# First x block and first two gates loaded and worked in halves, in a SwiGLU feed-forward kernel

## The chip, the cores and the metric

The kernel runs on one core of a Trainium2 chip. A time is that of one execution on the device in microseconds (us). The span in a profile runs from the first to the last instruction of the program, and times inside an execution are counted from the span's start.

## The reference

```python
B, S, D, F = 1, 2048, 512, 1376        # bf16; x, w_gate, w_up, w_down normal * 0.05

def reference(x, w_gate, w_up, w_down):
    g = silu(x @ w_gate)               # [S, F]
    u = x @ w_up                       # [S, F]
    return (g * u) @ w_down            # [S, D]
```

## The kernel before

Everything is held on chip. `xT_sb` has x transposed, as 4 blocks of 128 values of D (`dk` 0 to 3) by 2048 tokens; `w_sb` has the gate and up weights, `wd_sb` the down weights. F = 1376 is cut into 10 blocks of 128 (`ft`) and a rest of 96; the tokens are cut into 4 chunks of 512 (`SC`).

For each chunk and block there is one gate group G and one up group U, each a PSUM bank of 128 x 512 that sums over the 4 blocks of D. A 128-column weight block is worked as two 64-column halves side by side in the array (`m` 0 and 64), so matmuls come in pairs that run at the same time. ScalarE takes silu of G out of PSUM (L291), VectorE multiplies it with U (L305) into `hT_sb`. The rest of 96 is done in groups X and Y (L409, L420). Then the down projection runs over `hT_sb` (L456, L433) and the result is stored. The order of every engine's work is written out by hand: lists of groups, of ScalarE and of VectorE operations, with one counting semaphore for each of TensorE (`s_P`), ScalarE (`s_A`) and VectorE (`s_D`), and one semaphore for each load. `need(name)` makes TensorE wait for a load, `after(...)` for a ScalarE or VectorE operation.

What surrounds the change is the start:

- SP issues the loads in this order: `xn`, the first 256 tokens of x untransposed (256 KB, `HT` = 256); `wu0`, up columns 0 to 255 (256 KB); `x0b` and `x0c`, the next two 128 tokens by a transposing DMA; then slabs of gate and up weights, later chunks of x, and the down weights. ScalarE issues one load first of all: `wg0`, gate columns 0 to 255 (256 KB).
- TensorE runs `N_WARM` = 6 matmuls of constants, 512 wide (L359), and `N_FILL` = 2 pairs of 128 wide (L364). Then it waits for `xn` and transposes it: per block of D four transposes of 64 x 64 into a PSUM view `tview(dk)` for blocks 0 to 2 (L374), and four of 128 rows by 64 columns for the last block (L382). VectorE copies blocks 0 and 2 to `xT_sb`, ScalarE blocks 1 and 3 (L309, L291).
- Then come the first groups, on the first 256 tokens: gates 0 and 1 (`g0`, `g1`) block by block of D, 16 matmuls of 256 columns in all; ups 0 and 1 (`u0`, `u1`), 16 more; then `g0` on the tokens of `x0b` and `x0c`, the others on the rest. All these are L345.

`xn` holds tokens 2p and 2p + 1 in partition p, so that a token half of 128 is a half of 64 partitions. The list `turn` says which PSUM bank each group takes.

## Time and profile before

| | |
|---|---|
| time, median of 3 runs | 119.6 us (119.53 to 120.37) |
| time of the profiled execution | 120.67 us |
| its span | 119.3 us |
| TensorE (PE) busy | 116.6 us, 98% of the span |
| VectorE (DVE) busy | 43.4 us |
| ScalarE (ACT) busy | 35.5 us |
| granted TensorE clock | 1.00 |
| L345 matmuls | 680, 71.0 us |
| L359 and L364, matmuls of constants | 10, from 0.77 to 3.8 us |

The profile's chain of work is followed back from the last instruction, at each step to what released it. PE is TensorE's matmuls, PEld its weight loads, which lie beside them; SPq and ACTq are the queues of SP and ScalarE, whose lines show the issue of a DMA and not its transfer. A group's line has engine, operation, output and inputs with their shape, and the count. TensorE's first matmul starts 0.77 us after the span's start.

### The profile page before, as it was taken

The numbers are of one execution on the slowest core, as the hardware profiler recorded it, in microseconds if no ns is written. First come the engines' busy times: TensorE is split into PE (matmuls) and PEld (weight loads), VectorE is DVE, ScalarE is ACT, GpSimd is POOL, SyncE is SP. The second block draws the span as 40 slices with busy tenths as digits, with TensorE's granted clock in tenths as the row PEclk, the third lists the DMA queues.
The fourth block names the chain that finished last, engine by engine and source line by source line (L and its number), as shares of the span: only waits on it lengthen the run. The fifth ranks groups of instructions, "written<-read, shape, count | busy, mean of one in ns | idle before, by whom it ended". The sixth has DMA issues, their size and how long they took to land.

```text
span 119.3 us, 2992 instructions
## 1 busy us (share of the span) xinstructions
PE 116.6 (98%) x1343; PEld 66.4 (56%) x1344; DVE 43.4 (36%) x68; ACT 35.5 (30%) x61; POOL 0.4 (0%) x5
## 2 busy tenths in 40 slices
PE   7999999999999999999999999999999999999993
PEld 2796555555555555555555555554444444464452
DVE  0103534442534452444352444369800040214331
ACT  4225243265242365232454323470000030213001
POOL 1000000000000000000000000000000000000000
DMA  3999999991000000000000000000000023023612
GB/s 80 278 283 335 194 253 228 269 295 23 0 5 0 0 0 0 5 0 5 0 5 0 0 0 0 5 0 0 5 0 5 0 86 95 0 92 106 204 44 88
DMA packets 17596, 8.92 MB, mean 75 GB/s; under 512 B 8624, under 2 KB 17456, under 8 KB 17584
## 3 DMA queue, kind: packets, MB, share of 16 engines
q1 hardware_dynamic: 16912, 8.38, 27.1%
q10 hardware_dynamic: 672, 0.36, 1.0%
q8 instruction: 10, 0.16, 0.6%
q14 instruction: 2, 0.02, 0.0%
HBM read 4.81 MB, written 2.10 MB: 58 GB/s over the span
## 4 chain that ended last, share of the span: by engine, by line
PE 98%; issue 0%; DVE 0%
PE psum L345 59%; PE psum L456 24%; PE psum L433 7%; PE psum L409 3%; PE psum L359 2%; PE psum L420 1%; PE psum L382 0%; PE psum L374 0%; PE psum L364 0%; DVE o_sb L309 0%; PE psum L508 0%
## 5 line engine op out<-in xcount | busy, mean ns | idle before, releaser
L345 PE MATMUL psum<-xT_sb,w_sb 128*64 128x512 bf16 (+2 forms) x680 | 71.0, 371 | 0.0
L345 PEld LDWEIGHTS psum<-xT_sb,w_sb 128*64 128x64 bf16 x680 | 43.0, 112 | 27.1
L305 DVE TENSOR_TENSOR hT_sb<-sg_sb,psum 128x512 bf16<-128x512 f32 x40 | 27.5, 687 | 41.5 <-PE psum L345 36.6
L291 ACT ACTIVATE sg_sb<-psum 128x512 f32<-128x512 f32 x40 | 23.8, 596 | 41.6 <-PE psum L345 41.6
L456 PE MATMUL psum<-wd_sb,hT_sb 32*128 32x512 bf16 x480 | 26.9, 374 | 0.0
L456 PEld LDWEIGHTS psum<-wd_sb,hT_sb 32*128 32x128 bf16 x480 | 13.0, 93 | 13.0 <-issue 0.4
L309 DVE CAST o_sb<-psum 128x512 bf16<-128x512 f32 (+1 forms) x11 | 6.4, 603 | 25.2 <-PE psum L456 19.9
L291 ACT ACTIVATE o_sb<-psum 128x512 bf16<-128x512 f32 (+1 forms) x7 | 3.7, 580 | 33.0 <-PE psum L456 25.9
L433 PE MATMUL psum<-wd_sb,hT_sb 128*128 128x512 bf16 (+2 forms) x59 | 8.7, 307 | 0.2 <-issue 0.2
L433 PEld LDWEIGHTS psum<-wd_sb,hT_sb 128*128 128x128 bf16 x60 | 4.6, 98 | 4.6 <-issue 0.4
L305 DVE TENSOR_TENSOR ht_sb<-sgy_sb,yu_sb 32x512 bf16<-32x512 f32 x8 | 5.5, 683 | 0.4
L409 PE MATMUL psum<-xT_sb,w_sb 128*64 128x512 bf16 x32 | 4.2, 379 | 0.0
L305 DVE TENSOR_TENSOR ht_sb<-sgx_sb,psum 32x512 bf16<-32x512 f32 x4 | 2.8, 691 | 3.5 <-ACT sgx_sb L291 3.5
L291 ACT ACTIVATE sgx_sb<-psum 32x512 f32<-32x512 f32 x4 | 2.4, 588 | 4.5 <-PE psum L409 4.5
L359 PE MATMUL psum<-const-bfloat16-1.0 128*128 128x512 bf16 x6 | 2.7, 623 | 0.8 <-PEq L531 0.8
L456 PE MATMUL psum<-wdt_sb,ht_sb 32*128 32x512 bf16 (+1 forms) x48 | 3.3, 371 | 0.0
L409 PEld LDWEIGHTS psum<-xT_sb,w_sb 128*64 128x64 bf16 x32 | 2.0, 110 | 1.4
L291 ACT ACTIVATE sgy_sb<-psum 64x512 f32<-64x512 f32 x4 | 2.4, 590 | 0.1
L456 PEld LDWEIGHTS psum<-wdt_sb,ht_sb 32*128 32x128 bf16 x48 | 1.3, 93 | 1.3
L420 PE MATMUL psum<-xT_sb,w_sb 128*64 128x512 bf16 x16 | 1.9, 379 | 0.0
L359 PEld LDWEIGHTS psum<-const-bfloat16-1.0 128*128 128x128 bf16 x6 | 0.7, 133 | 1.9 <-issue 1.9
L280 ACT ACT_TABLE_LOAD x1 | 1.3, 1283 | 1.2 <-PEq L531 1.2
(21 smaller groups left out, 7.6 us busy)
## 6 DMA issues: line engine op xcount, KB each, us to landing
out_dram<-o_sb SPq DMA_DIRECT2D x15, 128.0 KB, 1.8
wd_sb<-in_w_down_dram SPq DMA_DIRECT2D x1, 1280.0 KB, 8.9
w_sb<-in_w_up_dram SPq DMA_DIRECT2D x4, 256.0 KB, 4.0
w_sb<-in_w_gate_dram SPq DMA_DIRECT2D x3, 256.0 KB, 3.9
wdt_sb<-in_w_down_dram SPq DMA_DIRECT2D x4, 96.0 KB, 7.2
w_sb<-in_w_gate_dram SPq DMA_DIRECT2D x1, 352.0 KB, 6.2
w_sb<-in_w_up_dram SPq DMA_DIRECT2D x1, 320.0 KB, 6.3
w_sb<-in_w_gate_dram ACTq DMA_DIRECT2D x1, 256.0 KB, 3.6
```

Source lines behind the costliest of these rows:

```text
L280: act.activation(adummy[:, 0:4], zero_c, ACT.Silu)
L291: act.activation(op["out"], op["src"], fn).then_inc(s_A, 1)
L305: ins = dve.tensor_tensor(op["out"], op["a"], op["b"], ALU.mult)
L309: ins = dve.tensor_copy(op["out"], op["src"])
L345: ins = pe.matmul(g["bank"][m:m + HC, n0:n1], lhsT=w_sb[:, dk, col + m:col + m + HC], rhs=xT_sb[:, dk, c * SC + n0:c * SC + n1], start=(dk ...
L359: pe.matmul(banks[NB - 1][:, 0:width], lhsT=ones_w, rhs=ones_m[:, 0:width], start=True, stop=True)
L409: ins = pe.matmul(g["bank"][m:m + HC, :], lhsT=w_sb[:, dk, XC0 + m:XC0 + m + HC], rhs=xT_sb[:, dk, c * SC:(c + 1) * SC], start=(dk == 0), ...
L420: ins = pe.matmul(g["bank"][y0:y1, :], lhsT=w_sb[:, dk, YC0:YC0 + 64], rhs=xT_sb[:, dk, c * SC:(c + 1) * SC], start=(dk == 0), stop=(dk == ...
L433: ins = pe.matmul(g["bank"][:, 0:c1 - c0], lhsT=hT_sb[:, fk, t * P:(t + 1) * P], rhs=wd_sb[:, fk, c0:c1], start=(start and fk == 0), stop= ...
L456: ins = pe.matmul(g["bank"][:, 0:c1 - c0], lhsT=h(r, g["t"]), rhs=w[R * r:R * (r + 1), c0:c1], start=(start and n == 0), stop=final, tile_ ...
```

## The change

The load of the first 256 tokens becomes two loads of 64 partitions (128 tokens, 128 KB each): `xn0` on SP in the old place, `xn1` on ScalarE's queue. The load `wg0` becomes `wg0a` (blocks 0 and 1 of D, 128 KB) and `wg0b` (blocks 2 and 3), both on ScalarE's queue, with `xn1` between them. `wu0` and all later loads keep their place on SP.

TensorE runs 4 matmuls of 512 and 3 pairs of 128 of constants. It then transposes the first half (8 transposes of 64 x 64), runs gates 0 and 1 on it for blocks 0 and 1 of D, transposes the second half, runs the gates on the first half for blocks 2 and 3, and then on the second half for all four. The gate matmuls of this part are 32 of 128 columns. The copies to `xT_sb` are one for each half and block: VectorE takes the first half's four and two of the second's, ScalarE the other two. All 4 blocks use the 64 x 64 form, and the list of banks is rearranged for it.

```diff
-N_WARM = 6
-N_FILL = 2
+N_WARM = 4
+N_FILL = 3
...
-        turn = [0, 2, 1, 3, 4, 5, 6, 7]
+        turn = [0, 4, 2, 6, 1, 3, 5, 7]
...
+        def load_rows(eng, h):
+            eng.dma_start(
+                xn_sb[h * HC:(h + 1) * HC, :, :].rearrange("p j d -> p (j d)"),
+                xf[h * P:(h + 1) * P, :].rearrange("(p j) d -> p (j d)", j=NXN),
+            ).then_inc(load_sem(f"xn{h}"), 16)
+
+        KH = KD // 2
...
         def loads_on_scalar(act):
-            load_w(act, "wg0", w_gate, 0, 0, slabs[0][1] * P)
+            load_w(act, "wg0a", w_gate, 0, 0, slabs[0][1] * P, 0, KH)
+            load_rows(act, 1)
+            load_w(act, "wg0b", w_gate, 0, 0, slabs[0][1] * P, KH, KD)
 
         def loads_on_sync(sp):
-            sp.dma_start(
-                xn_sb[:, :, :].rearrange("p j d -> p (j d)"), xf[0:HT, :].rearrange("(p j) d -> p (j d)", j=NXN)
-            ).then_inc(load_sem("xn"), 16)
+            load_rows(sp, 0)
             load_w(sp, "wu0", w_up, UPH, 0, slabs[0][1] * P)
             load_x(sp, "x0b", HT, HT + P)
...
+        def half(ap, h):
+            return ap.rearrange("p (i h t) -> p h i t", i=NXN, h=2)[:, h]
...
-        for dk in range(KD):
-            g = add_group("T", dk=dk)
-            eng = "DA"[dk % 2]
...
+        for h in range(2):
+            for dk in range(KD):
+                g = add_group("T", dk=dk)
+                eng = "A" if h and dk % 2 else "D"
+                op = add_op(
+                    eng, g, kind="copy", out=half(xT_sb[:, dk, 0:HT], h), src=tview(dk)[:, h], stored=(None, 0),
+                )
+                xt_ready[h, dk] = (eng, op["at"])
...
+            def transposes(h):
+                need(f"xn{h}")
+                if h == 0:
+                    pe.wait_ge(s_J, 1)
+                t0 = h * HC
+                for dk in range(KD):
+                    for i in range(NXN):
                         ins = pe.transpose(
                             tview(dk)[:, h, i, :], xn_sb[t0:t0 + HC, i, dk * P:(dk + 1) * P],
                             ident[t0:t0 + HC, t0:t0 + HC],
                         )
...
+                    ins.then_inc(s_P, 1)
+
+            def gate_part(h, dk0, dk1):
+                for g in (g0, g1):
+                    for dk in range(dk0, dk1):
+                        need("wg0a" if dk < KH else "wg0b")
+                        after(*xt_ready[h, dk])
+                        col = g["ft"] * P
+                        for m in (0, HC):
+                            pe.matmul(
+                                half(g["bank"][m:m + HC, 0:HT], h), lhsT=w_sb[:, dk, col + m:col + m + HC],
+                                rhs=half(xT_sb[:, dk, 0:HT], h), start=(dk == 0), stop=(dk == KD - 1),
+                                tile_position=(0, m),
+                            )
 
             g0, u0, g1, u1 = groups[NT:NT + 4]
-            for dk in range(KD):
-                for g in (g0, g1):
-                    gu_step(g, dk, 0, HT)
+            transposes(0)
+            gate_part(0, 0, KH)
+            transposes(1)
+            gate_part(0, KH, KD)
+            gate_part(1, 0, KD)
             for g in (u0, u1):
                 gu_matmuls(g, 0, HT)
```

More of the change, by code (lines that the diff above doesn't have):

```diff
@@ L95, in load_x, with load_w @@
             ).then_inc(load_sem(name), 16)
-        def load_w(eng, name, src, base, f0, f1):
+        def load_w(eng, name, src, base, f0, f1, k0=0, k1=KD):
             eng.dma_start(
-                w_sb[:, :, base + f0:base + f1],
-                src[:, f0:f1].rearrange("(k p) f -> p k f", p=P),
+                w_sb[:, k0:k1, base + f0:base + f1],
+                src[k0 * P:k1 * P, f0:f1].rearrange("(k p) f -> p k f", p=P),
             ).then_inc(load_sem(name), 16)
+        def load_rows(eng, h):
[4 more added lines that the diff above has]
+        KH = KD // 2
         slabs = [(0, 2), (2, 4), (4, 6), (6, 8), (8, NFT)]
@@ L140, in add_group @@
         def add_group(kind, **what):
-            g = dict(kind=kind, at=len(groups), bank=banks[turn[(len(groups) - KD) % NB]], readers=[], **what)
+            g = dict(kind=kind, at=len(groups), bank=banks[turn[(len(groups) - 2 * KD) % NB]], readers=[], **what)
             groups.append(g)
@@ L154, in tview @@
             return psum[:, 2 * dk:2 * dk + 2, 0:HC].bitcast(BF16).rearrange("p h (i t) -> p h i t", i=NXN)
-        def tview_last():
-            return psum[:, 6, 0:P].bitcast(BF16).rearrange("p (i t) -> p i t", i=NXN)
+        def half(ap, h):
+            return ap.rearrange("p (i h t) -> p h i t", i=NXN, h=2)[:, h]
         sg_reader = []
@@ L218, in bass_standalone__swiglu_ffn__prompt_kernel @@
         xt_ready = {}
-        for dk in range(KD):
-            g = add_group("T", dk=dk)
-            eng = "DA"[dk % 2]
-            out = xT_sb[:, dk, 0:HT]
-            if dk < KD - 1:
-                out, src = out.rearrange("p (i h t) -> p h i t", i=NXN, h=2), tview(dk)
-            else:
-                out, src = out.rearrange("p (i t) -> p i t", i=NXN), tview_last()
-            op = add_op(eng, g, kind="copy", out=out, src=src, stored=(None, 0))
-            xt_ready[dk] = (eng, op["at"])
+        for h in range(2):
[6 more added lines that the diff above has]
+                xt_ready[h, dk] = (eng, op["at"])
         NT = len(groups)
@@ L339, in gu_step @@
                     need("x0c")
-                need(("wg" if g["kind"] == "G" else "wu") + str(slab_of[ft]))
-                if c == 0 and n0 < HT:
-                    after(*xt_ready[dk])
+                side = ("a" if dk < KH else "b") if g["kind"] == "G" and slab_of[ft] == 0 else ""
+                need(("wg" if g["kind"] == "G" else "wu") + str(slab_of[ft]) + side)
                 col = (0 if g["kind"] == "G" else UPH) + ft * P
@@ L367, in on_tensor @@
                     )
-            need("xn")
-            pe.wait_ge(s_J, 1)
-            for dk in range(KD - 1):
-                for i in range(NXN):
-                    for h in range(2):
-                        t0 = h * HC
+            def transposes(h):
[5 more added lines that the diff above has]
+                    for i in range(NXN):
                         ins = pe.transpose(
@@ L377, in on_tensor @@
                         )
-                ins.then_inc(s_P, 1)
-            for i in range(NXN):
-                for m in (0, HC):
-                    c0 = (KD - 1) * P + m
-                    ins = pe.transpose(tview_last()[m:m + HC, i, :], xn_sb[:, i, c0:c0 + HC], ident[:, :])
-            ins.then_inc(s_P, 1)
-            g0, u0, g1, u1 = groups[NT:NT + 4]
-            for dk in range(KD):
-                for g in (g0, g1):
-                    gu_step(g, dk, 0, HT)
+                    ins.then_inc(s_P, 1)
[11 more added lines that the diff above has]
+                            )
+            g0, u0, g1, u1 = groups[NT:NT + 4]
+            transposes(0)
[3 more added lines that the diff above has]
+            gate_part(1, 0, KD)
             for g in (u0, u1):
```

## The prediction

> **What bounds the kernel now.** I read the page's chain first, then the chain in order of time, then the timeline of the first 9 us, then the DMA answers for short windows of the start.

> The chain, in order of time (start us, us, what):

> ```profile
> PE 98%; issue 0%; DVE 0%
> ...
> 0.77 2.72 PE psum L359 x6
> 3.49 0.33 PE psum L364 x3
> 3.82 0.33 PE psum L374 x11
> 4.15 0.36 PE psum L382 x4
> 4.51 18.56 PE psum L345 x200
> ```

> TensorE is the bound from 0.77 us to the end, without a hole. So the change can pay only in the first 6 us, where TensorE does work that isn't the result (L359, L364) because the loads aren't there yet. Everything later keeps its instructions and their order.

> The timeline of the start (start us, us, engine, line). The last five lines, from narrow windows, are pairs of weight loads of 256-column matmuls:

> ```profile
> 0.73 0.46 ACTq L98 DMA_DIRECT2D w_sb<-in_w_gate_dram  x1
> 0.74 0.41 SPq L114 DMA_DIRECT2D xn_sb<-in_x_dram  x1
> 1.20 0.41 SPq L98 DMA_DIRECT2D w_sb<-in_w_up_dram  x1
> 3.65 0.50 PE L374 MATMUL psum<-ident,xn_sb 64*128 64x64 bf16 x12
> 3.98 0.50 DVE L309 COPY xT_sb<-psum 128x256 bf16<-128x256 bf16 x2 [2.66 <-PE psum L374]
> 6.10 0.21 PEld L345 LDWEIGHTS psum<-xT_sb,w_sb 128*64 128x64 bf16 x2
> 6.31 0.21 PEld L345 LDWEIGHTS psum<-xT_sb,w_sb 128*64 128x64 bf16 x2
> 6.53 0.21 PEld L345 LDWEIGHTS psum<-xT_sb,w_sb 128*64 128x64 bf16 x2
> 6.90 0.22 PEld L345 LDWEIGHTS psum<-xT_sb,w_sb 128*64 128x64 bf16 x3
> 7.10 0.13 PEld L345 LDWEIGHTS psum<-xT_sb,w_sb 128*64 128x64 bf16 x2
> ```

> The DMA answers. First, issues and median us to landing; then the queues' packets in the windows 1.7 to 2.7, 3.25 to 3.55 and 4.0 to 4.3 us, in this order (q1 is SP's queue, q10 ScalarE's):

> ```profile
> w_sb<-in_w_gate_dram ACTq DMA_DIRECT2D x1, 256.0 KB, 3.6
> xn_sb<-in_x_dram SPq DMA_DIRECT2D x1, 256.0 KB, 2.9
> w_sb<-in_w_up_dram SPq DMA_DIRECT2D x1, 256.0 KB, 4.0
> ...
> q1 hardware_dynamic: 88, 0.18, 77.2%
> ...
> q10 hardware_dynamic: 200, 0.10, 112.5%
> q1 hardware_dynamic: 3, 0.00, 0.6%
> ...
> q1 hardware_dynamic: 206, 0.11, 115.9%
> q10 hardware_dynamic: 1, 0.00, 0.2%
> ```

> So xn lands at 0.74 + 2.9 = 3.6, wg0 at 0.73 + 3.6 = 4.3, wu0 at 1.20 + 4.0 = 5.2: 256 KB each 0.7 to 0.9 us after the one before. The two queues don't mix. wg0 is issued together with xn, yet up to 2.7 us only q1 moves; then q10 alone; and wu0, issued at 1.20, begins when wg0 is through. Transfers are served one after the other in the order of issue, whichever queue they are on.

> **The change part by part.** All sums are in us from the start of the span.

> *Warm-up.* Four 512-wide matmuls instead of six (their weight loads stand 0.427 apart, at 1.15, 1.58, 2.00 and 2.43) end at 0.77 + 1.71 = 2.48; three pairs of fill at 0.107 bring TensorE to 2.80, where it was 3.61.

> *x in halves.* 128 KB by the bytes moved: the windows 1.5 to 2.0 and 2.0 to 2.5 moved 41 and 72 KB (82 and 143 GB/s), so 128 KB are through at 2.57; the whole of xn was through at about 3.2 and landed at 3.6, 0.4 later, which gives 2.97 for xn0. By the slowest DMA engine it is later: eight 2 KB packets of 0.084 each end in a landing at 3.6, four of them 0.34 earlier, at 3.27. I take 3.1, so TensorE stands still from 2.80 to about 3.15. wg0a follows with another 128 KB at 340 GB/s: 3.5.

> *What comes next on the queues.* SP issues wu0 at 1.20 to 1.62, as before. ScalarE's second issue (xn1) can start when its first (0.46) is done, at about 1.23, and ends near 1.7; its third (wg0b) near 2.2. In the order of issue this is xn0, wg0a, wu0, xn1, wg0b: wu0 is past its slot by a few hundredths. The five together are the same 768 KB as xn, wg0 and wu0 before, so the last of them lands when wu0 did, at 5.2, and xn1 0.36 earlier, at 4.8. If xn1 beats wu0 it lands at 3.9, and wg0b is still at 5.2. Bounds for wg0b: 5.2 in the order of issue; 4.3 if ScalarE's three go ahead of wu0 (512 KB, where wg0 landed).

> *Transposes.* Still 16, but the 8 of a half use the same 64 rows of the array. In L374 they start in pairs 0.053 apart (0.50 less the 0.24 of one, over five steps); one behind the other, eight cost 0.42, the two halves 0.85, where the chain has 0.33 + 0.36 = 0.69 now. First half 3.15 to 3.57.

> *Copies.* Eight of 128 elements instead of four of 256. VectorE takes 0.29 for 256, and 0.23 for its 128-wide L299; I take 0.2. The first pair of transposes is out of the array 0.24 after its start (3.44), copied at 3.68; a matmul follows a copy by some 0.09. So the first gate matmuls start at 3.75, block 1's at 3.95, and the eight end at 4.28 (four pairs at 0.107, since 128-wide pairs take half of 0.213). Later copies lie beside the stalls below; VectorE has nothing else until 8.69. ScalarE's table load (1.28) moves from 1.23 to about 2.2 behind two more issues and ends at 3.5, before its first copy can be due.

> *The other halves.* xn1 at 4.8: TensorE stands still from 4.28 to 4.85, transposes to 5.27; wg0b has landed; eight matmuls to 5.70, sixteen more to 6.55. With xn1 at 3.9 the transposes run 4.28 to 4.70 and the stall comes behind them, up to 5.25: end 6.53. Now u0 starts at 6.10. The 32 matmuls of 128 have as many columns as 16 of 256; further on, at full rate, the 16 of 128x128 (0.6 us busy) keep half the spacing of the 256-wide, so splitting costs nothing, and the upper bound by weight loads alone is no more, since those lie beside them.

> *Nothing later.* wu0 lands by 5.2 at the latest and is needed at 6.55. Behind it SP's queue has the same bytes at the same times: x0b and x0c by 6.2. The new order of banks keeps reuse at eight groups' distance: no wait, covered by VectorE's and ScalarE's idle of 41 us each in front of L305 and L291.

> *Sum of the stalls.* 6.55 - 6.10 = 0.45 at half rate, 0.22 at full rate. If the rate doubles early, before 4.4, the gate work before ends at 5.27 (eight pairs at 0.107) and after the change at 5.20 + 0.21 + 0.43 = 5.84: 0.55. I take 0.3.

> *The rate.* The change puts holes into TensorE's first 6 us: 2.80 to 3.15, about 0.2 around the first copies, 4.28 to 4.85; 1.1 in all, of 2.4 us. Before, there is no hole from 0.77 to the doubling near 6.8, so 6.0 us of unbroken work suffice. How little would: the shown runs reach down to 119.53, the profiled execution took 120.67; were the 1.14 all the doubling's moment, it came 2.3 us earlier there, after 3.8. No row shows what a hole does. Lower bound: nothing, if holes up to half a microsecond don't count. Upper bound: the work before the last hole is lost and the count starts at 4.85 instead of 0.77, 4.1 us later, 2.0 at the end. With the first hole alone it starts at 3.15: 2.4 later, 1.2. I take 1.5, between those two, because the holes take almost half of the stretch that would have to count.

> [...]

> The profiled execution took 120.67 (span 119.3), 1.07 above the median of 119.6, and would become 122.5 by 0.3 + 1.5. The median of the runs: 119.6 + 0.3 + 1.5 = **121.4**.

> **The rivals.**

> *Stalls alone.* The doubling doesn't mind the holes. For it: none of them reaches 0.6 us. Against it: in 2.80 to 5.2 they are almost half. 119.6 + 0.2 to 0.55: about 119.95.

> *ScalarE's three loads are through before wu0.* Then the halves do what the description says: xn1 by 3.8, wg0b at 4.3, xn0 at 2.9 or so. Transposes 2.95 to 3.37, first gates to 4.1, second transposes to 4.52, sixteen and eight more to 5.8: 0.3 before 6.10, 0.15 to 0.35 at the end, and the holes are too small to matter: 119.35. Against it: the windows above, in which no queue gets a turn while the other has older work. It pays from wg0b's landing before about 4.8. [...]

> *x0's halves land late.* If xn0 takes as long as xn (3.6), the first hole is 0.8, the end of the gates stays at 6.55 by wg0b: no further cost but a surer late doubling, 121.6.

> **How the numbers follow.** The forecast (with the late x0) 0.53, stalls alone 0.29, ScalarE's loads early 0.18. Something over 1% (1.2 us, about what a measurement of this kernel can tell from no change) slower needs the late doubling: 0.53. Faster by so much needs a doubling that comes earlier as well, half of the third case at most: 0.08. Within 1%: 0.39. The range goes from the third case, 119.2, to the upper bounds less a little, 122.2; the forecast's own is 120.9 to 122.2.

> **What would show it.** Weight-load pairs 0.21 apart beyond 8 us, and TensorE idle in front of the second transposes or of the gates' blocks 2 and 3, with xn1 or wg0b landing near 5: right. Pairs 0.11 apart by 7 us in most executions: stalls alone. wu0 landing after wg0b, and gates ended before 6.1: the third case. Holes of 1 us with a doubling no later than 6.8 would make the forecast wrong.

## The result and the profile after

The changed kernel takes 123.36 us in the median (123.26 to 123.56, 6 runs), the kernel before 119.62 (119.48 to 120.37, 6 runs beside it): ratio 1.030, 95% interval 1.026 to 1.033. It is slower by 3.7 us; the prediction said 121.4, at most 122.2. (The ratios and intervals leave out executions that lie over 1.5% above a kernel's fastest, the medians and ranges don't; where a kernel's times fall into two groups, I give the times.)

The chain of the changed kernel (first the page's shares, then in order of time: start us, us, what):

```profile
PE 93%; DMA 4%; ACTq 1%; DVE 0%; issue 0%
...
0.74 0.41 ACTq L98
1.15 0.03 issue
1.18 0.55 ACTq L104
1.73 0.04 issue
1.77 4.83 DMA w_sb<-in_w_gate_dram
6.60 0.04 issue
6.64 1.49 PE psum L394 x24
8.14 17.51 PE psum L350 x183
```

Before, the chain was TensorE from 0.77 on. Now its first 6.6 us are ScalarE's three issues and the transfer of wg0b, which takes 4.83 from its issue. From 8 us on the pieces have the lengths they had.

The timeline (issues; TensorE's matmuls; weight-load pairs from narrow windows), then the answers on landing (KB, us from issue):

```profile
0.74 0.41 ACTq L98 DMA_DIRECT2D w_sb<-in_w_gate_dram  x1
0.74 0.57 SPq L104 DMA_DIRECT2D xn_sb<-in_x_dram  x1
1.18 0.55 ACTq L104 DMA_DIRECT2D xn_sb<-in_x_dram  x1
1.36 0.57 SPq L98 DMA_DIRECT2D w_sb<-in_w_up_dram  x1
...
3.86 0.60 PE L381 MATMUL psum<-ident,xn_sb 64*128 64x64 bf16 x8 [0.79 <-DMA xn_sb<-in_x_dram]
4.55 0.64 PE L394 MATMUL psum<-xT_sb,w_sb 128*64 128x128 bf16 x8
5.22 0.61 PE L381 MATMUL psum<-ident,xn_sb 64*128 64x64 bf16 x8
6.64 1.49 PE L394 MATMUL psum<-xT_sb,w_sb 128*64 128x128 bf16 x24 [0.82 <-DMA w_sb<-in_w_gate_dram]
...
9.85 0.28 PEld L350 LDWEIGHTS psum<-xT_sb,w_sb 128*64 128x64 bf16 x4
10.31 0.17 PEld L350 LDWEIGHTS psum<-xT_sb,w_sb 128*64 128x64 bf16 x4
```

```profile
w_sb<-in_w_gate_dram ACTq DMA_DIRECT2D x1, 128.0 KB, 2.5
xn_sb<-in_x_dram SPq DMA_DIRECT2D x1, 128.0 KB, 3.1
...
xn_sb<-in_x_dram ACTq DMA_DIRECT2D x1, 128.0 KB, 4.0
...
w_sb<-in_w_up_dram SPq DMA_DIRECT2D x1, 256.0 KB, 5.0
w_sb<-in_w_gate_dram ACTq DMA_DIRECT2D x1, 128.0 KB, 4.8
```

wg0a lands at 3.3, xn0 at 3.8, xn1 at 5.2, wu0 at 6.4, wg0b at 6.6. The half of x lands later than the whole did (3.6). TensorE has holes of 1.1, 0.2, 0.2 and 1.0 us, counted by its weight loads; the matmuls, whose ends the profile models, show 0.79 and 0.82 for the two long ones. The pairs of 128 columns are 0.107 apart up to 10.1 and half of that behind it (four weight loads take 0.28 at 9.85 and 0.17 at 10.31): the rate doubles at 10.2, 3.4 after the 6.7 of the profiled execution before. Pairs still 0.21 apart beyond 8 us were one of the prediction's signs, and it came.

wg0b's landing has two parts. Its last packet ended at 5.58 by the trace's records, and from 5.65 to 6.6 us only SP's queue moved packets (packets, MB, share of 16 engines):

```profile
q1 hardware_dynamic: 498, 0.13, 84.4%
```

So the landing came 1.0 behind the last packet; before, wg0's came 0.3 behind (4.01 and 4.33). In that stretch packets on SP's queue, most of them x0b's, waited too, up to 1.0 us and until 6.1. Nothing on record tells the cause.

**Where the time went.** Let U be the start of u0, the end of the start phase, and L the first matmul at full rate, both read from the records of single matmuls. Everything behind U is the same work, at half rate up to L. So the span should be a constant plus U, or plus (U + L)/2 where L is later than U. With a constant of 112.9, chosen to fit, it is so within 0.1 us in 12 of the 16 profiled executions:

| kernel | U | L | by the formula | span | median time (range) |
|---|---|---|---|---|---|
| before | 6.10 | 6.74 | 119.3 | 119.3 | 119.62 (119.48 to 120.37) |
| changed | 7.93 | 10.17 | 121.9 | 121.9 | 123.36 (123.26 to 123.56) |
| hole_alone | 6.02 | 6.02 | 118.9 | 119.0 | 121.05 (120.32 to 121.75) |
| no_warm | 6.07 | 6.92 | 119.4 | 119.4 | 121.23 (120.74 to 121.97) |
| first_filled | 6.88 | 4.11 or earlier | 119.8 | 120.5 | 121.70 (121.25 to 121.93) |
| after_filled | 6.73 | 4.11 | 119.6 | 119.6 | 121.49 (121.04 to 123.32) |
| loads_alone | 6.49 | 4.71 or earlier | 119.4 | 119.4 | 122.14 (120.71 to 123.08) |
| compute_split | 5.88 | 4.46 | 118.8 | 118.8 | 121.12 (120.06 to 122.63) |
| wg_halves | 6.09 | 5.98 | 119.0 | 119.0 | 120.23 (119.92 to 120.34) |
| single_transposes | 6.13 | 6.56 | 119.2 | 119.2 | 119.77 (119.52 to 120.59) |
| halves_128 | 6.86 | 9.64 | 121.1 | 121.1 | 122.03 (120.31 to 122.50) |
| halves_128_filled | 6.12 | 5.42 | 119.0 | 119.1 | 121.23 (120.30 to 123.31) |
| halves_timely | 5.86 | 5.52 | 118.8 | 119.0 | 120.70 (120.21 to 121.47) |
| xn_on_sp | 7.61 | 11.03 | 122.2 | 122.2 | 122.92 (122.24 to 123.85) |
| one_queue | 8.11 | 10.57 | 122.2 | 122.2 | 123.52 (123.41 to 124.66) |
| x0b_waits | 7.11 | 10.40 | 121.7 | 121.9 | 123.29 (123.11 to 123.64) |

A time is the span and some 1.35. In first_filled the rest of 0.7 lies behind TensorE's last matmul, in the last stores, and so do the smaller rests of halves_timely and halves_128_filled; in x0b_waits it lies in a hole of 0.5 behind U. In first_filled, after_filled and loads_alone L is read from the transposes: at full rate those of 64 columns start 0.03 us apart instead of 0.053.

Between the two profiled executions U is 1.83 later, worth 0.91, and L 3.43 later, worth 1.71: 2.62 of the 2.59 by which the spans differ. The medians differ by 3.74, because in the profiled execution before the rate doubled late and it took 1.05 more than the median. The kernel before's lowest times, 119.5 again and again, are what the formula gives if the rate doubles before the gates start at 4.42: U is then 4.42 + 0.85 = 5.27 (eight pairs at 0.107, half of the 0.213 seen there; an estimate), and 112.9 + 5.27 + 1.35 = 119.52. No such execution of the kernel before was profiled.

### The profile page after: what moved, and what is told of

It reads as the page before. It is cut to its first block, busy times and chain, and to the rows that moved or that the text cites. A ratio compares the mean times of both kernels' runs of the same rounds, so it can differ in the third digit from the quotient of the medians.

```text
span 121.9 us, 3032 instructions
## 1 busy us (share of the span) xinstructions
PE 117.6 (96%) x1360; PEld 61.9 (51%) x1360; DVE 44.0 (36%) x72; ACT 35.2 (29%) x61; POOL 0.4 (0%) x5
## 4 chain that ended last, share of the span: by engine, by line
PE 93%; DMA 4%; ACTq 1%; DVE 0%; issue 0%
PE psum L350 57%; PE psum L473 23%; PE psum L450 7%; DMA w_sb<-in_w_gate_dram 4%; PE psum L426 3%; PE psum L437 1%; PE psum L394 1%; ACTq L104 0%; ACTq L98 0%; DVE o_sb L315 0%; PE psum L525 0%
## 5 line engine op out<-in xcount | busy, mean ns | idle before, releaser
L350 PE MATMUL psum<-xT_sb,w_sb 128*64 128x512 bf16 (+2 forms) x664 | 70.0, 374 | 0.0
L350 PEld LDWEIGHTS psum<-xT_sb,w_sb 128*64 128x64 bf16 x664 | 37.4, 113 | 31.7
L426 PE MATMUL psum<-xT_sb,w_sb 128*64 128x512 bf16 x32 | 4.1, 379 | 0.0
L394 PE MATMUL psum<-xT_sb,w_sb 128*64 128x128 bf16 x32 | 2.1, 314 | 0.9 <-DMA w_sb<-in_w_gate_dram 0.8
L426 PEld LDWEIGHTS psum<-xT_sb,w_sb 128*64 128x64 bf16 x32 | 1.8, 110 | 1.7
L364 PE MATMUL psum<-const-bfloat16-1.0 128*128 128x512 bf16 x4 | 1.9, 619 | 0.8 <-PEq L548 0.8
L315 DVE COPY xT_sb<-psum 128x128 bf16<-128x128 bf16 x6 | 1.1, 220 | 3.6 <-PE psum L381 3.6
L394 PEld LDWEIGHTS psum<-xT_sb,w_sb 128*64 128x64 bf16 x32 | 1.7, 167 | 1.2 <-DMA w_sb<-in_w_gate_dram 1.0
L381 PE MATMUL psum<-ident,xn_sb 64*128 64x64 bf16 x16 | 1.2, 238 | 0.8 <-DMA xn_sb<-in_x_dram 0.8
## 6 DMA issues: line engine op xcount, KB each, us to landing
w_sb<-in_w_up_dram SPq DMA_DIRECT2D x4, 256.0 KB, 4.5
w_sb<-in_w_gate_dram SPq DMA_DIRECT2D x3, 256.0 KB, 4.0
```

The costliest lines, as they stand in the source:

```text
L315: ins = dve.tensor_copy(op["out"], op["src"])
L350: ins = pe.matmul(g["bank"][m:m + HC, n0:n1], lhsT=w_sb[:, dk, col + m:col + m + HC], rhs=xT_sb[:, dk, c * SC + n0:c * SC + n1], start=(dk ...
L364: pe.matmul(banks[NB - 1][:, 0:width], lhsT=ones_w, rhs=ones_m[:, 0:width], start=True, stop=True)
L381: ins = pe.transpose(tview(dk)[:, h, i, :], xn_sb[t0:t0 + HC, i, dk * P:(dk + 1) * P], ident[t0:t0 + HC, t0:t0 + HC],)
L394: pe.matmul(half(g["bank"][m:m + HC, 0:HT], h), lhsT=w_sb[:, dk, col + m:col + m + HC], rhs=half(xT_sb[:, dk, 0:HT], h), start=(dk == 0), ...
L426: ins = pe.matmul(g["bank"][m:m + HC, :], lhsT=w_sb[:, dk, XC0 + m:XC0 + m + HC], rhs=xT_sb[:, dk, c * SC:(c + 1) * SC], start=(dk == 0), ...
```

## Experiments

Each was run beside the kernel before. First the rate, then the loads, then both repaired.

**hole_alone.** The kernel before, with the changed warm-up.

```diff
-N_WARM = 6
-N_FILL = 2
+N_WARM = 4
+N_FILL = 3
```

> The kernel before with 4 matmuls of 512 and 3 pairs of 128 of constants (N_WARM 4, N_FILL 3) instead of 6 and 2; loads and everything else as before. xn still lands at 3.6 us, so TensorE stands still from 2.80 to 3.65 and nothing else moves. Theory 'the hole puts off the doubling of TensorE's rate': gates start at 4.4 as before, pairs of matmuls stay 0.21 apart until well beyond 6.9 us, up to 10.3; median 120.6 to 122.4. Rival 'stalls of loads are all that costs': no start moves, 119.6 within 0.3.

Median 121.05 against 119.70, 1.35 more; ratio 1.010 (1.007 to 1.013). The gates start when they did:

```profile
0.74 2.79 DMA xn_sb<-in_x_dram
3.52 0.05 issue
3.57 0.50 PE psum L374 x11
4.07 0.36 PE psum L382 x4
4.43 2.58 PE psum L345 x29
```

The first line is now a wait where the constants were. A hole of 0.75 that delays nothing costs 1.35 in the median here. The profiled execution (L 6.0) was the fastest of ten, so that the rate doubles later in the others is not seen but worked out: by the formula the median of 121.05 has L near 7.6 (an estimate).

**no_warm.** The kernel before without any constants.

```diff
-N_WARM = 6
-N_FILL = 2
+N_WARM = 0
+N_FILL = 0
```

> The kernel before without any matmuls of constants (N_WARM 0, N_FILL 0): TensorE starts with the transposes at 3.65, gates at 4.4 as before. Theory 'a hole of 0.75 makes the count start anew': the 2.0 us of work ahead of the hole in the kernel with the hole alone were worth nothing, so both take the same, 120.8 to 121.4. Rival 'work ahead of a hole counts in part': later than the hole alone by up to half of 2.0, 121.5 to 122.2.

121.23 against 120.01, ratio 1.011 (1.005 to 1.016). That is 0.18 from hole_alone's median, and the intervals overlap: these runs show no worth of the 2.0 us of work ahead of hole_alone's hole. That it never counts isn't shown: in hole_alone's fastest execution the rate doubled 2.45 us after the hole's end, in no_warm's fastest 3.3 us after the first transpose.

**after_filled and first_filled.** The changed kernel with all holes filled by constants, or the first one alone.

```diff
# both
-N_WARM = 4
-N_FILL = 3
+N_WARM = 6
+N_FILL = 5
...
# after_filled only; fill(n, ...) runs n matmuls of constants, 128 wide, on each half that it names
             gate_part(0, 0, KH)
+            fill(3, (1,), (7,))
             transposes(1)
+            after(*xt_ready[0, 2])
+            after(*xt_ready[0, 3])
+            fill(9, (0, 1), (4, 6))
             gate_part(0, KH, KD)
```

> The changed kernel with its holes filled by matmuls of constants: 6 of 512 and 5 pairs of 128 at the start (to 3.87, xn0 landed at 3.82), three of 128 ahead of the second transposes, nine pairs of 128 (0.96 us) ahead of blocks 2 and 3 of D. Loads unchanged, so the gates should end where they did, near 7.9. Theory 'holes put off the doubling': it comes at 4.6 to 6.9 as in the kernel before instead of 10.2, half of 3.3 to 5.6 is won: 120.6 to 121.7. Rival 'the 64-row and 128-column instructions themselves don't count': doubling stays near 10, 123.3.

> The changed kernel with its first hole alone filled (6 matmuls of 512 and 5 pairs of 128 of constants, to 3.87); the holes in front of the second transposes and of blocks 2 and 3 of D stay. Theory 'the count starts anew behind the last hole': nothing is won, 123.0 to 123.6. [...]

after_filled: 121.49, ratio 1.013 (1.005 to 1.021), with one of its four times at 123.32. first_filled: 121.70, ratio 1.014 (1.009 to 1.018), with all four times below 122 and a spread of 0.7. Filling one hole, with the stalls left in, wins 1.7 of the 3.7. The timeline of first_filled:

```profile
4.11 0.41 PE L381 MATMUL psum<-ident,xn_sb 64*128 64x64 bf16 x8
4.75 0.41 PE L394 MATMUL psum<-xT_sb,w_sb 128*64 128x128 bf16 x8 [0.23 <-DVE xT_sb L315]
5.10 0.40 PE L381 MATMUL psum<-ident,xn_sb 64*128 64x64 bf16 x8
6.19 0.86 PE L394 MATMUL psum<-xT_sb,w_sb 128*64 128x128 bf16 x24 [0.69 <-DMA w_sb<-in_w_gate_dram]
```

The eight gate matmuls take 0.41 where the changed kernel's took 0.64, and the eight transposes ahead of them 0.41 where it was 0.60: the rate has doubled by 4.11, while the constants up to 3.83 are still 0.1 apart. It stays doubled through the hole up to 6.19. So "the count starts anew behind the last hole" fell as a general rule: a hole of 0.7 to 0.9 us behind the doubling didn't undo it here. The first hole is what keeps the changed kernel from doubling early (L 10.17 with it, 4.11 or earlier without). Whether its last hole puts the doubling off further, from some 7.6 as in hole_alone to 10.2, no run shows by itself.

**compute_split.** The changed kernel's work with the loads and the warm-up of before.

```diff
-N_WARM = 4
-N_FILL = 3
+N_WARM = 6
+N_FILL = 2
...
-            load_w(act, "wg0a", ...); load_rows(act, 1); load_w(act, "wg0b", ...)
+            load_w(act, "wg0", w_gate, 0, 0, slabs[0][1] * P)
...
-            load_rows(sp, 0)
+            sp.dma_start(xn_sb ..., xf[0:HT, :] ...)     # whole xn
```

> The changed kernel's TensorE, VectorE and ScalarE work with the loads of before (xn whole on SP, wg0 whole on ScalarE's queue) and the warm-up of before (6 and 2). Theory 'the loads and the holes cost, not the split of the work': xn at 3.6, wg0 at 4.3, one hole of 0.2 around the first copies, gates end 0.2 later than before's 6.1, doubling as before: 119.5 to 119.9. Rival 'smaller instructions hold the clock back': doubling near 10, about 122.

Two groups: five times from 120.06 to 120.30, five from 121.94 to 122.63 (interval of the first against before: 0.999 to 1.006). Inconclusive as to my bounds: with an early doubling the split costs about half a microsecond over before's 119.5; in the other half, 2.2 longer, U would be near 6.8 at half rate and the doubling by the formula near 9.4 (estimates), some 5 us later, after a hole of no more than 0.3 in the profiled execution. So the split, or the small hole that comes with it, seems to put the doubling off in some executions, and why stays open.

**single_transposes.** Before's L374 without pairs.

```diff
-                for i in range(NXN):
-                    for h in range(2):
+                for h in range(2):
+                    for i in range(NXN):
```

> The kernel before with L374's transposes in another order: for each block the two of the first 64 rows, then the two of the other 64, instead of alternating, so that they don't run in pairs; nothing else. Theory 'what counts towards the doubling is how much of the array works, so single 64-row transposes count for half': 0.1 later start of the gates (3 blocks, 0.1 each at most), but in a part of the executions the doubling comes 3.4 later, as in the kernel with the work's split alone: some times of 119.6 and some of 121.5 to 122.5. Rival 'only holes count': 119.5 to 120.8 in all.

119.77 against 119.77, ratio 1.000 (0.996 to 1.003): no late group. Pairs or single transposes made no difference here, and compute_split's two groups stay unexplained. (For the theory's 3.4 there is the distance between the L of the two profiled executions, 6.74 and 10.17; that compute_split's later group doubles 3.4 later, no run shows.)

**loads_alone.** The kernel before with the changed kernel's loads.

```diff
# the four loads as in the change; besides
-            need("xn")
+            need("xn0")
+            need("xn1")
...
-                need(("wg" if g["kind"] == "G" else "wu") + str(slab_of[ft]))
+                side = ("a" if dk < KH else "b") if g["kind"] == "G" and slab_of[ft] == 0 else ""
+                need(("wg" if g["kind"] == "G" else "wu") + str(slab_of[ft]) + side)
```

> The kernel before with the changed kernel's loads (xn0, xn1, wg0a, wg0b on the two queues) and its own TensorE work and warm-up (6 and 2): all transposes wait for xn0 and xn1, the gates for wg0a and wg0b block by block. Theory: xn1 lands at 4.3 to 5.2, wg0b at 5.8 to 6.6, so a hole from 3.6 to 4.8 and one up to 6.2 in front of blocks 2 and 3; gates end 6.9 to 7.5; doubling beyond 8: 122 to 124, all of the change's loss without its split of the work. Rival 'the split of the work is half of the loss': under 121.5.

122.14 against 119.77, times from 120.71 to 123.08, ratio 1.017 (1.009 to 1.025): 2.4 of the 3.7 by the medians, without any split of the work. xn0 landed at 4.1, xn1 at 4.6, wg0b at 6.0. In the profiled execution, the fastest of four, the transposes at 4.71 run at full rate, behind a hole of 1.1 us. So a hole like that doesn't put the doubling off in every execution; that it did in the other three, 121.86 to 123.08, is worked out from their times alone (an estimate).

**x0b_waits.** Nothing transposes while wg0b is on its way.

```diff
+            sp.wait_ge(wg0b_sem, 16)
             load_x(sp, "x0b", HT, HT + P)
```

> The changed kernel, but SP waits for wg0b's landing before it issues x0b, so that no transposing transfer is under way while wu0, xn1 and wg0b move. Theory 'x0b's transposing transfer, issued on SP at 2.0 us, held up wg0b and part of wu0 (5.0 to 6.1 us, 100 GB/s)': wg0b lands near 5.2 instead of 6.6, gates end near 6.6 instead of 7.9, half of 1.3 won: 122.7, or less if the doubling moves too. Rival 'the two queues' plain loads hold each other up': wg0b stays at 6.6; 123.4 or more, as x0b comes later.

123.29, no gain. wg0b landed at 5.8; but with the changed kernel's very loads it landed at 5.9 in after_filled, 6.1 in first_filled and 6.6 in the changed kernel's profile, so the 0.8 is within what differs between executions. x0b came late and made a hole of its own at 9.3, which took back what the earlier U (7.11) won, so the time can't tell either. The theory isn't borne out, and isn't excluded.

**xn_on_sp and one_queue.** Other queues for the same loads.

```diff
# xn_on_sp
             load_rows(sp, 0)
+            load_rows(sp, 1)          # and not on ScalarE
# one_queue
             load_rows(sp, 0)
-            load_w(sp, "wu0", w_up, UPH, 0, slabs[0][1] * P)
+            load_w(sp, "wg0a", w_gate, 0, 0, slabs[0][1] * P, 0, KH)
+            load_rows(sp, 1)
+            load_w(sp, "wg0b", w_gate, 0, 0, slabs[0][1] * P, KH, KD)
# ScalarE, once xn0 has landed; its table load moves ahead of this wait
+            act.wait_ge(xn0_sem, 16)
+            load_w(act, "wu0", w_up, UPH, 0, slabs[0][1] * P)
```

> The changed kernel with xn1 on SP behind xn0; ScalarE's queue has wg0a and wg0b only, SP xn0, xn1, wu0, x0b and on. Theory 'two queues run into each other': still two queues with five loads, so late: wg0a 3.3, xn0 3.8, wg0b and xn1 between 4.5 and 5.3, gates end 6.2 to 6.9, doubling after 9: 121.5 to 123. Rival 'it is only xn1 and wg0b queued behind each other on ScalarE's slow issue': wg0b by 4.4, xn1 by 4.7, gates by 6.2, under 121.2.

> The changed kernel with the four half loads on one queue in the order of need: SP issues xn0, wg0a, xn1, wg0b, then x0b, x0c and the slabs as before; ScalarE issues wu0 alone, once xn0 has landed. Theory 'the halves come late because two queues' loads run into each other and a short wg0a gets ahead of xn0': served one after the other, xn0 lands near 3.0, wg0a 3.5, xn1 3.9, wg0b 4.4; the gates end near 6.0, holes are 0.3 and 0.2, the doubling comes as in the kernel with the hole alone or earlier: 119.3 to 121.0 (x0b, x0c and the slabs land 1.0 later than before, which may cost 0.2). Rival 'a load on 64 partitions is slow in itself': wg0b beyond 5.2 again, over 122.

xn_on_sp: 122.92, ratio 1.026 (1.020 to 1.031); xn0 at 4.5, xn1 at 5.6. one_queue: 123.52, ratio 1.035 (1.029 to 1.042); xn0 at 3.5 although nothing was ahead of it, xn1 4.8, wg0b 6.2. Its wu0 landed at 8.1, which my order is to blame for. So two queues running into each other was not needed to make xn0 and xn1 late: in order on one queue, xn1 came 1.1 behind wg0a. For wg0b this run can't tell, since wu0 on the other queue began (4.87) before it landed. The rival stood, that the loads on 64 partitions are slow in themselves (xn0, first and alone, took 2.8 us to landing).

**halves_128.** The same halves, one token in each of 128 partitions.

```diff
-                xn_sb[h * HC:(h + 1) * HC, :, :].rearrange("p j d -> p (j d)"),
-                xf[h * P:(h + 1) * P, :].rearrange("(p j) d -> p (j d)", j=NXN),
+                xn_sb[:, h, :], xf[h * P:(h + 1) * P, :],
...
-                            tview(dk)[:, h, i, :], xn_sb[t0:t0 + HC, i, dk * P:(dk + 1) * P], ident[...]
+                        ins = pe.transpose(tview(dk, h)[m:m + HC, :], xn_sb[:, h, c0:c0 + HC], ident[:, :])
```

> The changed kernel with each x half spread over all 128 partitions (one token of 1 KB in each) instead of 64 partitions of 2 KB; the transposes become pairs of 128 rows by 64 columns, 16 as before, and the first two output tiles are stored in plain order. Queues and order of issue unchanged. Theory 'loads on 64 partitions are slow (issue 0.57 instead of 0.41, and half of the memory's partitions to write to)': xn0 lands by 3.4, xn1 by 4.0, wg0b by 5.0; the first two holes shrink to 0.5 and 0.2, gates end by 6.5, 120.3 to 121.8. Rival 'five transfers where there were three, whatever their shape': wg0b between 5.7 and 6.6, 122.5 to 123.5.

The load of xn0 in one_queue, first on its queue, and then in halves_128 (queue, duration of the issue; us to landing):

```profile
L105 SPq DMA_DIRECT2D xn_sb<-in_x_dram x1: 566/566/566, 0.7 to 0.7; - x1
...
DMA to landing us min/median/max: 2.8/2.8/2.8
```

```profile
L104 SPq DMA_DIRECT2D xn_sb<-in_x_dram x1: 400/400/400, 0.7 to 0.7; - x1
...
DMA to landing us min/median/max: 2.3/2.3/2.3
```

On 64 partitions the issue takes 0.17 longer and the landing 0.45. By the packet records the transfer itself isn't longer: in one_queue xn0's packets run from 2.10 to 2.87, in halves_128 from 1.78 to 2.70. They begin 0.32 later, and the landing comes 0.62 behind the last packet instead of 0.35. In the changed kernel the longer issue also lets wg0a pass: its packets begin at 1.80, xn0's at 2.30, and xn0 lands 3.1 after its issue. The bytes moved in the windows of 1 us from 2.5 and from 3.5, of before, of the changed kernel and of halves_128 (last column GB/s):

```profile
2.50:3.50 1.00, 1.00 (x5) 1.00 0.91 302
3.50:4.50 1.00, 1.00 (x22) 1.00 1.16 344
```

```profile
2.50:3.50 1.00, 0.57 (x7) 1.00 0.94 240
3.50:4.50 1.00, 0.60 (x8) 1.00 0.98 258
```

```profile
2.50:3.50 1.00, 0.98 (x15) 1.00 0.98 254
3.50:4.50 1.00, 0.87 (x14) 1.00 1.12 343
```

With 128 partitions the rate of before is back in the second window, though not in the first. In the second window the seven profiled kernels with loads on 64 partitions moved 174 to 285 GB/s, the nine others 308 to 344. halves_128 takes 122.03 in the median: 120.31 and three from 121.82 to 122.50 (interval 1.000 to 1.018); the profiled one is of the late ones. xn0 landed at 3.05, wg0a 3.41, xn1 4.77, wu0 4.98, wg0b 5.54: U at 6.86. That lies between the theory and its rival: all loads but wg0a land earlier than in the changed kernel, and xn1 and wg0b later than the theory said. Why loads on 64 partitions go with the lower rate (258 against 343 GB/s), no run here shows.

**wg_halves.** Before, with wg0 alone in halves.

```diff
-            load_w(act, "wg0", w_gate, 0, 0, slabs[0][1] * P)
+            load_w(act, "wg0a", w_gate, 0, 0, slabs[0][1] * P, 0, KH)
+            load_w(act, "wg0b", w_gate, 0, 0, slabs[0][1] * P, KH, KD)
... (and the gates' waits)
```

> The kernel before with wg0 alone as two loads of 128 KB on ScalarE's queue (blocks 0 and 1, then 2 and 3 of D); xn whole on SP, TensorE's work as before. Theory 'the 64-partition halves of x are what comes late': xn 3.6, wg0a 3.9 to 4.0, wg0b 4.4, gates as before: 119.5 to 120.0. Rival 'more transfers cost': wg0b mixes with wu0 and lands at 5.0 or later, gates wait 0.4 or more: 120.2 to 121.5.

120.23 against 120.01, ratio 1.002 (0.997 to 1.006): no cost that the interval shows. wg0a landed at 3.9, wg0b at 5.3, where blocks 2 and 3 were due in any case at half rate. But wg0b came 0.9 later than the theory's 4.4, and its fastest time of four is 119.92, where before reaches 119.5: where the rate doubles early, wg0b at 5.3 is too late (blocks 2 and 3 would be due at 4.42 + 0.43 = 4.85 there, an estimate). And the last of the loads, wu0, landed at 5.67 instead of 5.17, with the same bytes and no load on 64 partitions. So more transfers cost something too, as the rival said. The queues from 4.2 to 4.8 us:

```profile
q1 hardware_dynamic: 478, 0.14, 103.5%
q10 hardware_dynamic: 100, 0.04, 25.3%
```

Both move at once here, which the prediction's windows of before didn't show.

**halves_128_filled and halves_timely.** halves_128 with a warm-up up to xn0, and that with both x halves on SP ahead of wu0.

```diff
-N_FILL = 3
+N_FILL = 6
# halves_timely only
             load_rows(sp, 0)
+            load_rows(sp, 1)          # and not on ScalarE
```

> halves_128 with 6 pairs of fill instead of 3 (to 3.1), so that no hole is in front of the first transposes; loads as there (xn1 4.8, wg0b 5.5), holes of 0.25, 0.5 and 0.3 stay. [...] Rival 'the hole of 0.3 was too short to matter': 122.0.

> Halves of x on 128 partitions, both on SP ahead of wu0; ScalarE's queue has wg0a and wg0b; 4 matmuls of 512 and 6 pairs of 128 of constants (to 3.1, where xn0 landed with such halves). Theory 'late loads and holes are the whole loss': xn0 3.05, wg0a 3.4, xn1 3.8, wg0b 4.2 to 4.4; gates from 3.8, one behind the other up to 6.0; holes of 0.25 around the first copies only; 119.4 to 120.3, no gain over before beyond 0.2. Rival 'the split itself costs': over 121.

halves_128_filled: 121.23, times from 120.30 to 123.31, ratio 1.009 (1.005 to 1.013), in the median 0.8 under the 122.0 of its rival (the ranges of the two kernels overlap); the profiled execution doubled at 5.4. halves_timely: 120.70, ratio 1.006 (1.003 to 1.009), over its bound by 0.4. Its loads came as laid out (3.1, 3.5, 3.9, 4.2), and the chain has no transfer in it:

```profile
3.40 0.27 PE psum L378 x2
3.66 0.02 issue
3.69 0.36 DVE xT_sb L312 x2
4.05 0.01 issue
4.05 0.64 PE psum L388 x8
4.69 0.43 PE psum L378 x8
5.12 0.92 PE psum L388 x24
```

The gates start 0.37 earlier than before's 4.42, but the second half's transposes (0.43) and the wait for the copies (0.36) now lie on TensorE's chain, and the rate doubled at 5.5 in this execution, one of the fastest of ten. So late loads and holes are most of the loss, not all: in time, the halves end U 0.24 before the profiled execution before, and the times are still 0.6% longer. No version beat the kernel before.

## Why the prediction was wrong

- **What bounds the kernel, and the worth of the start:** right. Nothing behind u0 changed, and the half worth of the slow part is what makes the table's formula.
- **xn0 at 3.1:** wrong, 3.8, and wg0a before it. That half the bytes take half the time held roughly for the packets, which took 0.80 where xn's took 1.41. What failed is that they would begin when xn's did (1.77) and land 0.4 behind the last: on 64 partitions they began at 2.30, behind an issue of 0.57 and behind wg0a, and landed 0.7 behind. On 128 partitions it landed at 3.05.
- **wg0b at 5.2, since the five loads are the same 768 KB:** the step that failed most, 6.6. The total was right and the rate was not: 258 GB/s where before had 344, from 3.5 to 4.5 us. That accounts for about half of the 1.4: the last packet ended at 5.6, 0.7 later than a landing at 5.2 allows, and the landing came 0.7 later behind it than wg0's had, for a reason that stays open. With halves_128 the summed landings hold within 0.1 for xn0, wg0a and xn1, and wg0b is 0.3 late; in wg_halves, too, the same bytes were not through by 5.2. The reading "one after the other in the order of issue" was drawn from three loads of one execution; wg_halves shows two queues moving together, and so does before itself from 3.58 to 4.0 us (0.08 MB on ScalarE's queue, 0.06 on SP's), when wu0 had begun and wg0 was not through.
- **Stalls, 0.3:** U came 1.83 late, not 0.45. Worth 0.9 at half rate, and 1.6 where the rate has doubled early (6.88 in first_filled against 5.27). first_filled's wg0b landed 0.46 earlier than the changed kernel's; with 6.60, and the 0.74 from there to U as in first_filled, U would be 7.34, and the stalls 2.1 (an estimate). The prediction's own sum for this case was 0.55; the 1.4 by which wg0b is late makes the rest.
- **The doubling, 1.5:** that the holes put it off was right (L 10.17 against 6.74, and 4.11 with the holes filled), and the size near. From an early doubling with U at 7.34 to the changed kernel's U of 7.93 and L of 10.17 the formula gives (7.93 + 10.17)/2 - 7.34 = 1.7 (an estimate). With the stalls' 2.1 that is 3.8, where the medians differ by 3.74: the forecast's shortfall lies in the stalls, not here. hole_alone shows a hole's price by itself, 1.35. My upper bound of 2.0 hung on the last hole ending at 4.85; it ended at 6.64, and the rate doubled 3.5 behind it. That a last hole always wipes out the work before it was refuted by first_filled.
- **Split at no cost:** not quite. halves_timely and the earlier group of compute_split are 0.5 to 1 above before, and compute_split's later group 2.5.
- **The rivals:** "stalls alone" is excluded by L. "ScalarE's loads early" didn't happen. "x0's halves land late" was what happened, and I had priced it at only 0.2 over the forecast because I took wg0b's landing for fixed.

The moment of the doubling seems not to be fixed in a kernel. hole_alone's ten times spread over 1.4 us, which the formula puts down to it (an estimate). The changed kernel's six times lie within 0.3. What sets the moment, no run here tells.

## What to carry to other kernels

If a load is cut in two, halve the bytes in each partition, not the partitions: half of x landed later than the whole (3.6) on 64 partitions, at 3.8, and earlier on 128, at 3.05. Even then it is not half as long (2.3 us to landing instead of 2.9), and more transfers can put off the last landing (wu0 at 5.67 instead of 5.17 in wg_halves). Where the array starts at half rate, as it did here (pairs 0.213 us apart up to 6.5 and 0.11 from 6.9 in before), a hole in the start can cost twice, once as a stall (U 7.93 instead of 6.10) and again by a later full rate (L 10.17 instead of 6.74), so warm-up work has to reach the first load's landing with certainty; look at the spacing of matmuls, since the granted clock read 1.00 at both rates. When a start is tuned to landings, count the issues too: each took 0.4 to 0.6 us of its queue here.

## What the runs showed of the hardware that I had not expected

- 128 KB on 64 partitions from an idle start landed 2.8 us after its issue (one_queue) and on 128 partitions 2.3 (halves_128); 256 KB on 128 partitions 2.9 (before).
- Once doubled, the rate stayed so through a hole of 0.7 to 0.9 us (first_filled), while a hole of 0.75 ahead of the doubling cost 1.35 in the median (hole_alone). The earliest doubling that a trace dates came 3.3 us after the first matmul, without a hole (after_filled, 4.11).
- Transposes follow the rate too: of 64 columns, they start 0.053 us apart up to the doubling and 0.03 behind it (after_filled).
- The same five loads differed by up to 1.1 us in landing between four executions (xn1 4.3 to 5.2, wu0 5.3 to 6.4, wg0b 5.9 to 6.6). From 5.1 to 6.1 us packets of the changed kernel waited up to 1 us; x0b's transposing transfer was not shown to be the cause, and it stays open.
